# Reordering the first loads of a cross-layer kernel: the transposing load second on its queue, W0 on the other, no filler between the input halves

## The chip, the cores and the metric

One core of one Trainium2 chip runs the whole program. The metric is the time of one execution in microseconds on the device, with inputs and outputs in device memory. Fast runs of the kernel before spread over up to 1.5 per cent on one chip (131.16 to 133.06 us in 31 runs). Each run also lists the mean granted clock of TensorE over the span (1.00 is full). A run is called slow here when it took over 1.5 per cent longer than the fastest run of the same kernel; medians are of all runs, ratios of the fast ones alone.

## The reference

Six cross layers on a batch of 4096 rows with 416 features, in bf16:

```python
x = x0                                  # x0 [4096, 416]
for l in range(6):                      # ws [6, 416, 416], bs [6, 416]
    x = x0 * (x @ ws[l] + bs[l]) + x
```

## The kernel before: the parts that matter

Rows are processed in four slabs of 1024. Features are split into three chunks of 128 and a tail of 32. The activations are needed transposed (features on partitions). For slab 0 the first 512 rows come in plainly as two halves `xin` and are transposed on TensorE; rows 512 to 1023 come by one transposing DMA into `x0T_sb`. All of these first loads share two hardware queues (SP and ACT) and one software queue (POOL):

```python
# SP
sp.dma_start(xin_sb[:, 0:2, :], x0_v[:, 0:2, :]).then_inc(s_xin[0], 16)
sp.dma_start(w_sb[:, 0, 0, :], ws[0, 0:128, :]).then_inc(s_w0, 16)
sp.dma_start_transpose(x0T_sb[:, :, H:SB], x0[H:SB, 0:DF]).then_inc(s_x0T[0], 16)
for l in range(1, L):                       # W1 .. W5 and the tail rows of their weights
    ...
# ACT
act.dma_start(xin_sb[:, 2:4, :], x0_v[:, 2:4, :]).then_inc(s_xin[1], 16)
act.dma_start(w_sb[:, 0, 1:NC, :], ...).then_inc(s_w[0], 16)      # W0, blocks 2 and 3
act.dma_start(xtl_sb[:, 4:JS, :], ...).then_inc(s_xtl0, 16)       # tail input
act.dma_start(bsa_sb[1:L + 1, :], bs[:, :]).then_inc(s_bs, 16)    # bias rows
for g in (1, 3):
    load_wt(act, g, 0, 1, s_wt[0])                                # tail weights of layer 0
```

TensorE works through the start of layer 0 in program order: 13 filler matmuls (their results are not used), transposes of input half 0, three fillers, transposes of half 1, step k=0 (needs W0 block 1), step k=1 (needs W0 blocks 2 and 3), bias sums (need the bias rows), tail transposes (need the tail input), step k=2, then the tail group of matmuls, then half B of the slab (needs the transposing load):

```python
for k in range(NC):
    if k == 1:
        pe.wait_ge(s_w[0], 16)
    if k == 2:
        bias_sums()                  # waits for s_bs
        pe.wait_ge(s_xtl0, 16)
        tail_transposes(0)
    before_a(k)
    for m in range(NC):
        step(m, 0, k)
...                                  # tail group, then
pe.wait_ge(s_x0T[0], 16)
```

## Time and profile before

| | before |
|---|---|
| time, median of the first three runs | 131.67 us (131.44 to 132.03) |
| span of the profiled run, TensorE busy | 130.2 us, 125.0 us |
| first matmul of layer 0 | 6.10 us |
| first tail group (called T below) | 9.09 us |
| one layer afterwards | 4.88 us |
| W0 blocks 2 and 3: issue, landing | 1.34, 5.64 us |
| transposing load: issue, landing | 1.82, 9.02 us |

All moments are microseconds from the start of the span. A landing is the issue's start plus the time to landing that the DMA view gives. From T on the kernel keeps a fixed rhythm, so only the first ten microseconds are of interest here; the lines that show it stand in the prediction.

In the profile, PE is the row of TensorE's matmuls and PEld that of its weight loads; DVE is VectorE, ACT ScalarE, POOL GpSimd, SP SyncE, and a q behind a name marks what was issued to its DMA queue. One pair of lines belongs here because the prediction read another line in its place. This is the timeline of TensorE's matmuls in the kernel before (start, length, engine, line, operation; a bracket at the end would name an idle time and its releaser):

```profile
6.10 1.81 PE L194 MATMUL ps<-x0T_sb,w_sb 128*32 128x512 bf16 x24
7.84 0.26 PE L194 MATMUL ps<-u_sb,bsa_sb 7*32 7x6 bf16 x16
```

There is no bracket: the matmuls of k=0 and k=1 run until 6.10 + 1.81 = 7.91, and the bias sums follow without a gap (the profile models the ends of matmuls, hence the small overlap). No wait for the bias rows shows.

### The profile page before, as it was taken

The numbers are of one execution on the slowest core, as the hardware profiler recorded it, in microseconds if no ns is written. First come the engines' busy times: TensorE is split into PE (matmuls) and PEld (weight loads), VectorE is DVE, ScalarE is ACT, GpSimd is POOL, SyncE is SP. The second block draws the span as 40 slices with busy tenths as digits, with TensorE's granted clock in tenths as the row PEclk, the third lists the DMA queues.
The fourth block names the chain that finished last, engine by engine and source line by source line (L and its number), as shares of the span: only waits on it lengthen the run. The fifth ranks groups of instructions, "written<-read, shape, count | busy, mean of one in ns | idle before, by whom it ended". The sixth has DMA issues, their size and how long they took to land.

```text
span 130.2 us, 5402 instructions
## 1 busy us (share of the span) xinstructions
PE 125.0 (96%) x2456; PEld 65.0 (50%) x2456; DVE 99.6 (76%) x151; ACT 68.8 (53%) x157; POOL 21.9 (17%) x39
## 2 busy tenths in 40 slices
PE   6999999999999999999999999999999999999970
PEld 4655545545545545545545545545445545545540
DVE  2319779779779779779779779779779779779780
ACT  0615456566905456565905556565905555555680
POOL 7302012012022022012022022012022032012230
PEclk9999999999999999999999999999999999999999
DMA  3999799960009935000008534000009707000026
GB/s 100 232 264 352 77 202 221 162 146 0 5 3 105 158 106 167 5 0 5 0 5 161 106 111 156 0 5 0 5 0 118 154 0 262 5 0 5 0 86 184
DMA packets 34018, 11.95 MB, mean 92 GB/s; under 512 B 26694, under 2 KB 33996, under 8 KB 33996
## 3 DMA queue, kind: packets, MB, share of 16 engines
q1 hardware_dynamic: 32160, 10.91, 40.9%
q10 hardware_dynamic: 1708, 0.64, 1.9%
q8 instruction: 19, 0.31, 0.9%
q0 software_dynamic: 128, 0.06, 0.2%
q14 instruction: 3, 0.02, 0.1%
HBM read 2.90 MB, written 3.41 MB: 48 GB/s over the span
## 4 chain that ended last, share of the span: by engine, by line
PE 96%; ACT 0%; POOL 0%; issue 0%; POOLq 0%
PE ps L194 81%; PE ps L328 10%; PE ps L201 3%; PE ps L226 1%; PE ps L381 1%; ACT o_sb L503 0%; POOL ones_sb L153 0%; POOLq L522 0%
## 5 line engine op out<-in xcount | busy, mean ns | idle before, releaser
L427 DVE SCALAR_TENSOR_TENSOR xT_sb<-ps,cb_sb,x0T_sb 128x512 bf16<-128x512 f32 x120 | 80.9, 743 | 16.9 <-PE ps L328 16.9
L194 PE MATMUL ps<-xT_sb,w_sb 128*32 128x512 bf16 (+1 forms) x1680 | 89.3, 364 | 0.0
L194 PEld LDWEIGHTS ps<-xT_sb,w_sb 128*32 128x32 bf16 x1680 | 42.8, 97 | 38.7 <-issue 4.2
L475 ACT ACTIVATE t_sb<-ps,cb_sb 64x256 f32<-64x256 f32 x48 | 22.6, 470 | 35.6 <-PE ps L194 35.2
L457 ACT ACTIVATE xt_sb<-xt_sb 32x256 bf16<-32x256 bf16 x80 | 33.1, 414 | 14.4 <-POOL xt_sb L181 13.6
L181 POOL TENSOR_TENSOR xt_sb<-t_sb,x0t_sb 128x256 bf16<-128x256 f32 x20 | 13.5, 676 | 83.0 <-ACT t_sb L475 83.0
L194 PE MATMUL ps<-x0T_sb,w_sb 128*32 128x512 bf16 (+1 forms) x336 | 18.8, 369 | 0.0
L427 DVE SCALAR_TENSOR_TENSOR xo_sb<-ps,cb_sb,x0T_sb 128x512 bf16<-128x512 f32 x23 | 15.6, 744 | 3.4 <-PE ps L328 3.3
L194 PEld LDWEIGHTS ps<-x0T_sb,w_sb 128*32 128x32 bf16 x336 | 8.6, 98 | 7.9 <-issue 1.6
L328 PE MATMUL ps<-xt_sb,wt_sb 32*128 32x512 bf16 (+1 forms) x160 | 12.1, 326 | 0.0
L328 PE MATMUL ps<-xt_sb,wc_sb 32*128 32x256 bf16 x80 | 7.7, 268 | 0.0
L328 PEld LDWEIGHTS ps<-xt_sb,wt_sb 32*128 32x128 bf16 x160 | 2.4, 91 | 8.5 <-DVE xT_sb L427 8.5
L457 ACT ACTIVATE x0t_sb<-x0t_sb 32x256 bf16<-32x256 bf16 x12 | 5.0, 414 | 0.2
L181 POOL TENSOR_TENSOR xot_sb<-t_sb,x0t_sb 128x256 bf16<-128x256 f32 x4 | 2.7, 675 | 13.5 <-ACT t_sb L475 13.5
L201 PE MATMUL ps<-ones_sb 128*128 128x256 bf16 x16 | 3.8, 419 | 1.2 <-POOL ones_sb L153 1.2
L328 PEld LDWEIGHTS ps<-xt_sb,wc_sb 32*128 32x128 bf16 x80 | 4.0, 93 | 0.4
L405 DVE COPY x0T_sb<-ps 128x256 bf16<-128x256 bf16 x4 | 1.2, 292 | 3.3 <-PE ps L226 3.1
L446 ACT ACT_TABLE_LOAD x1 | 1.3, 1283 | 3.9 <-issue 3.9
L201 PEld LDWEIGHTS ps<-ones_sb 128*128 128x128 bf16 x16 | 2.2, 146 | 1.9 <-POOL ones_sb L153 1.2
L328 PE MATMUL ps<-x0t_sb,wt_sb 32*128 32x512 bf16 (+1 forms) x32 | 2.4, 326 | 0.0
L483 ACT ACTIVATE x0t_sb<-ps 64x256 bf16<-64x256 f32 x6 | 2.3, 378 | 0.1
L409 DVE CAST x0t_sb<-ps 128x256 bf16<-128x256 f32 x1 | 0.4, 425 | 2.1 <-PE ps L194 2.1
(38 smaller groups left out, 25.5 us busy)
## 6 DMA issues: line engine op xcount, KB each, us to landing
out_dram<-o_sb SPq DMA_DIRECT2D x3, 832.0 KB, 4.2
w_sb<-in_ws_dram SPq DMA_DIRECT2D x5, 312.0 KB, 4.6
out_dram<-o_sb SPq DMA_DIRECT2D x2, 256.0 KB, 2.5
xin_sb<-in_x_dram SPq DMA_DIRECT2D x1, 208.0 KB, 3.0
xin_sb<-in_x_dram ACTq DMA_DIRECT2D x1, 208.0 KB, 3.3
w_sb<-in_ws_dram ACTq DMA_DIRECT2D x1, 208.0 KB, 4.3
xtl_sb<-in_x_dram SPq DMA_DIRECT2D x1, 192.0 KB, 7.0
wt_sb<-in_ws_dram SPq DMA_DIRECT2D x2, 80.0 KB, 4.0
```

Of the source, the lines that this page charges most:

```text
L181: pool.tensor_tensor(out=dst, in0=t32_sb[:, n % 2, :], in1=x0t_sb[:, s, 0:G], op=ALU.mult).then_inc(s_xt, 1)
L194: return pe.matmul(dst, lhsT=lhsT, rhs=rhs, start=start, stop=True, skip_group_check=True, tile_position=(0, 32 * q),)
L201: pe.matmul(ps[:, 7, 0:256], lhsT=ones_sb[:, 0:128], rhs=ones_sb[:, :], start=True, stop=True)
L226: ins = pe.transpose(out=psT[:, IN_BANKS[h][c], (j % 2) * 128:(j % 2 + 1) * 128], in_=xin_sb[:, j, c * 128:(c + 1) * 128], identity=ident[ ...
L328: return pe.matmul(dst, lhsT=lhsT, rhs=srct[lane(g), cols], start=l == 0 and start, stop=True, skip_group_check=True, tile_position=(32 * ...
L381: return pe.transpose(out=psT[:, bank, slot * 128:(slot + 1) * 128], in_=xo_sb[:, NS - 1, c, j * 128:(j + 1) * 128], identity=ident[:, :],)
L405: dve.tensor_copy(out=x0T_sb[:, c, h * 256:(h + 1) * 256], in_=psT[:, IN_BANKS[h][c], 0:256]).then_inc(s_inD, 1)
L427: dve.scalar_tensor_tensor(out=dst, in0=ps[:, NC * half + c, :], scalar=cb_sb[:, c, l:l + 1], in1=x0T_sb[:, c, o:o + H], op0=ALU.add, op1= ...
L446: act.activation(out=x0T_sb[:, 1, h * 256:(h + 1) * 256], in_=psT[:, IN_BANKS[h][1], 0:256], func=ACTF.Copy).then_inc(s_inA, 1)
L457: ins = act.activation(out=buf[lane(g), G:2 * G], in_=buf[lane(g ^ 1), 0:G], func=ACTF.Copy)
L475: ins = act.activation(out=t32_sb[HALVES[h], n % 2, :], in_=tail(h), func=ACTF.Identity, bias=cb_sb[HALVES[h], NC, l:l + 1],)
L483: ins = act.activation(out=x0t_sb[HALVES[h], s + 1, 0:G], in_=spare(h), func=ACTF.Copy)
```

## The change

Its intent is to have the transposing load, the largest of the first loads, land earlier by issuing it as the second load of SP. W0's first block therefore goes to ACT, where the bias rows move to the end. With more issues on ACT, one PSUM copy moves from ACT to VectorE. The filler between the input halves goes. On POOL the small tail-by-tail weights are split by layer and follow the tail weights.

```diff
 # SP
-            sp.dma_start(w_sb[:, 0, 0, :], ws[0, 0:128, :]).then_inc(s_w0, 16)
             sp.dma_start_transpose(x0T_sb[:, :, H:SB], x0[H:SB, 0:DF]).then_inc(s_x0T[0], 16)
 # ACT
             act.dma_start(xin_sb[:, 2:4, :], x0_v[:, 2:4, :]).then_inc(s_xin[1], 16)
+            act.dma_start(w_sb[:, 0, 0, :], ws[0, 0:128, :]).then_inc(s_w0, 16)
             act.dma_start(w_sb[:, 0, 1:NC, :], ...).then_inc(s_w[0], 16)
             act.dma_start(xtl_sb[:, 4:JS, :], x0_v[:, 4:JS, DF:D]).then_inc(s_xtl0, 16)
-            act.dma_start(bsa_sb[1:L + 1, :], bs[:, :]).then_inc(s_bs, 16)
             for g in (1, 3):
                 load_wt(act, g, 0, 1, s_wt[0])
+            act.dma_start(bsa_sb[1:L + 1, :], bs[:, :]).then_inc(s_bs, 16)
 # TensorE, after the transposes of half h
-                fill((3, 0)[h])
 # VectorE copies of half 0: chunks (0, 2) -> (0, 1, 2); ACT keeps only chunk 1 of half 1
-                            pe.wait_ge((s_inD, s_inA, s_inD)[k], (3, 2, 4)[k])
+                            pe.wait_ge((s_inD, s_inA, s_inD)[k], (4, 1, 5)[k])
 # POOL: wc load split into layer 0 and layers 1 to 5, after the tail weights; TensorE waits for it by layer  (cut)
```

## The prediction

> **What bounds the kernel now.** I read the busy table first, then the chain of work that ended last, then the waits of the first 14 us, then the timeline and DMA issues of that stretch. The first two, from the page:
>
> ```profile
> PE 125.0 (96%) x2456; PEld 65.0 (50%) x2456; DVE 99.6 (76%) x151; ACT 68.8 (53%) x157; POOL 21.9 (17%) x39
> ...
> PE 96%; ACT 0%; POOL 0%; issue 0%; POOLq 0%
> ```
>
> TensorE is busy nearly all the time and is 96% of the chain that ends last. The chain in order of time shows where layer 0 hands over to a regular rhythm:
>
> ```profile
> 5.41 0.64 PE ps L226 x6
> 6.10 3.00 PE ps L194 x67
> 9.09 0.56 PE ps L328 x8
> 9.66 4.33 PE ps L194 x84
> 13.98 0.55 PE ps L328 x8
> 14.53 4.33 PE ps L194 x84
> ```
>
> Columns: start, length, what. From the first tail group (9.09) on, each layer takes 4.89 us (13.98 - 9.09, and 18.86 - 13.98 = 4.88 later), which the diff does not touch. So the change moves the end only by what it moves that 9.09. I call this moment T. The waits before it, each with total, count and longest in us:
>
> ```profile
> DVE x0t_sb L409 <- PE ps L194: 2.1, 1, 2.1
> ACT cb_sb L450 <- PE ps L194: 1.9, 1, 1.9
> ...
> PEld ps L194 <- DMA bsa_sb<-in_bs_dram: 0.4, 1, 0.4
> PEld ps L328 <- ACT x0t_sb L461: 0.4, 1, 0.4
> ```
>
> There is one DMA wait on the PE path before T: the bias rows. The timeline around it (start, length, engine, line, operation, then idle before and releaser):
>
> ```profile
> 2.39 0.66 ACTq L441 DMA_DIRECT2D bsa_sb<-in_bs_dram  x1
> 3.07 0.80 ACTq L107 DMA_DIRECT2D wt_sb<-in_ws_dram  x2
> ...
> 7.84 0.17 PEld L194 LDWEIGHTS ps<-u_sb,bsa_sb 7*32 7x32 bf16 x16 [0.42 <-DMA bsa_sb<-in_bs_dram]
> ...
> 8.51 0.38 ACT L461 ACTIVATE x0t_sb<-ps 128x256 bf16<-128x256 f32 x1
> ...
> 9.02 0.14 PEld L328 LDWEIGHTS ps<-x0t_sb,wt_sb 32*128 32x128 bf16 x8 [0.42 <-ACT x0t_sb L461]
> ```
>
> Bias rows issued at 2.39 release PE at about 7.84, so 5.4 us. From there everything is a chain: bias sums, tail transposes, the ACT copy 8.51 to 8.89, tail weights at 9.02. T follows the landing of the bias rows by 1.2 us (9.02 - 7.84).
>
> Last, the issues to landing, from DMA views of narrow stretches (size, us):
>
> ```profile
> xin_sb<-in_x_dram ACTq DMA_DIRECT2D x1, 208.0 KB, 3.3
> w_sb<-in_ws_dram ACTq DMA_DIRECT2D x1, 208.0 KB, 4.3
> xtl_sb<-in_x_dram ACTq DMA_DIRECT2D x1, 32.0 KB, 4.6
> wt_sb<-in_ws_dram ACTq DMA_DIRECT2D x1, 8.0 KB, 4.9
> wt_sb<-in_ws_dram ACTq DMA_DIRECT2D x1, 8.0 KB, 5.3
> x0T_sb<-in_x_dram SPq DMA_TRANSPOSE x1, 7.2
> ```
>
> Everything issued after 1.7 us takes about 5 us, even 8 KB: the small loads stand in a backlog, of which the transposing load (issued 1.82, landed 9.02) is the largest part.
>
> **What the Trainium skill says.** "DMA: Bandwidth & Descriptors", section "Issuing engines are not separate DMA queues": loads from SP, ACT and POOL run on the same 16 DMA engines and interleave; a second issuing engine saves only issue time. The trace agrees: an 8 KB load of ACT takes 4.9 us and a 16 KB one of POOL 5.0 to 5.1. The same page, section "Queues, rings and completion order": an engine takes its rings in turn by packets and each ring in order. The order within ACT's ring is visible (input, W0, tail input, bias, tail weights land in issue order); the fair turn is not, since POOL's almost empty ring waits as long.
> "TensorE: Matmul & The Clock Gate", Part 1: the array runs at half rate until it has been busy for a free-running window of about 3.4 us. The trace agrees: six 128-column transposes take 0.64 us, 107 ns each (the page's cold figure), and the four-way 512-column groups of layer 0 start about 0.40 us apart (weight loads at 6.07, 6.48, 6.87) and then 0.21. It became fast near 6.9 us.
>
> **The change part by part.**
> 1. The filler between the halves goes: three matmuls, 0.64 us in the chain (4.77 to 5.41). The second input half landed at 0.82 + 3.3 = 4.12, so its transposes can follow at 4.77 and end at 5.41, not 6.05: 0.64 us earlier on PE.
> 2. The half-0 chunk-1 copy moves from ACT to VectorE. VectorE now has five copies of 0.29 us. Chunk 0 starts at 4.38 as before; back to back the fourth, which step k=0 needs, ends at 4.38 + 4 x 0.29 = 5.55, the fifth at 5.84. Before, k=0 waited for the third copy, at 5.66 + 0.29 = 5.95, and began at 6.10. So k=0 can begin near 5.7: a gain of 0.4 us, not 0.64.
> 3. W0's first block moves from SP to ACT, behind the input. Landed at 1.33 + 3.0 = 4.33; now it shares the engines with the transpose for longer, and I expect 4.8 to 5.5, just in time for 5.7. The two other blocks, 1.34 + 4.3 = 5.64 before, go to about 6.3; k=1 wants them at 6.9. ACT's own table load (1.28 us) starts after its last issue, at 4.4 instead of 3.9, its remaining copy ends near 6.1: also ahead of k=1.
> 4. The transposing load is issued 0.49 us earlier (1.33), landing near 8.5 instead of 9.02. PE asks for it at about 9.6. No wait on it is shown, so nothing gained now, only slack.
> 5. The bias rows go behind W0's block (0.49 us) and both tail-weight issues (0.80 us): 2.39 + 1.29 = 3.68. The last small load of that kind issued late (3.45) took 5.3 us, and ahead of 3.68 stands most of the transpose, whose issuing takes 2.73 us (now until 4.06). With 5.1 us they land at 8.8, against 7.84: 0.95 us later. This is on the path.
> 6. The lane-weight loads split in two and stand behind POOL's tail weights: 4 x 0.67 us of issue, from 2.5 to 5.2. Layer 0's pair, issued by 3.8, lands by 8.8; layer 1's has until 14. The small select for the bias sums moves from 4.08 to 5.2, still early. Cost: nothing.
>
> The sum: k=0 and k=1 start 0.4 us earlier and only wait longer for the bias rows (parts 1 and 2 give nothing). T = 8.8 + 1.2 = 10.0 in place of 9.02: +0.95 us. Then the fixed rhythm. 131.67 + 0.95 is 132.6; I take 132.5, since a backlog with W0's and the input's bytes unchanged may let the bias rows through a little sooner.
>
> **The rivals.**
> A. The intended gain: the bias rows are not late because the ACT ring's last load finds the transpose further along, or rings are served fairly. If they land by 7.4, PE never waits and the whole 0.4 us (at most 0.64) is kept: 131.1 to 131.3. For it: the transpose starts half a microsecond earlier. Against: no small load of any queue got through in under 4.6 us.
> B. The clock: without filler PE idles some 0.3 us before k=0 and 1 us or more at the bias wait. If the window then counts as idle, the array stays slow for one more window of 3.4 us; half of that is lost, up to 1.7 us, on top of the 0.95: 134.3. Against: most of each window remains busy (about 70% of 7 to 10.2), and no slow stretch after 6.9 is in the trace before.
> C. The transpose starves W0: the second and third blocks land at 7.5 or later and step k=1 waits. That stays hidden under the wait for the bias rows unless it passes 8.1 (8.8 less the 0.64 us of a fast k=1): no more than 0.5 us extra, 133.
>
> **Range and chances.** The main step gives +0.6 to +1.2 (latency of 4.75 to 5.35 us); A takes the low end to 131.2, B and C the high end to 133.7. The three runs before span 131.44 to 132.03, so the noise is near 0.3 us. Two per cent is 2.63 us: a gain of that size exceeds all of the stretch that can be saved (0.64), a loss needs the backlog and a cold clock together. Faster 0.01, same 0.93, slower 0.06. Prediction 132.5 us, range 131.2 to 133.7.
>
> **What would show it.** Part 1 and 2: layer 0's first matmul near 5.7 instead of 6.10. Part 5: the bias weight load starts near 8.8 with an idle of over 1 us put down to the bias DMA. The first tail group near 10.0, then layers 4.88 us apart. Part 4: transposing load landing near 8.5 with no wait on it. The clock: groups of layer 0 0.21 us apart from about 7 us. I am wrong if the bias rows land before 8.0, if PE waits for W0 or the transpose instead, or if the layer rhythm after T is not 4.88.

## The result, and the profile after

The changed kernel took 136.72 us (median; 135.35 to 138.00, 4 runs, of which the one at 138.00 is slow) against 131.65 us (131.44 to 132.03, 4 runs). The ratio is 1.0347, with a 95% interval of 1.0266 to 1.0428: slower. Ratios here are the mean time of one kernel's fast runs over that of the other's fast runs of the same rounds, so not quite the ratio of the medians quoted.

The chain that ended last, in order of time, of the changed kernel (start, length, what):

```profile
4.11 5.86 DMA bsa_sb<-in_bs_dram
10.02 2.11 PE ps L194 x39
12.12 0.97 PE ps L328 x8
13.10 5.55 PE ps L194 x72
18.64 0.55 PE ps L328 x8
19.19 4.33 PE ps L194 x84
```

T moved from 9.09 to 12.12, the next tail group from 13.98 to 18.64; after that the rhythm is the old one. All of the loss lies ahead of 18.64: 18.64 - 13.98 = 4.66 us, and the spans differ by 134.9 - 130.2 = 4.7. A load now heads this chain. The waits of the first 14 us (total, count, longest):

```profile
PEld ps L194 <- DMA w_sb<-in_ws_dram: 2.4, 1, 2.4
PE ps L194 <- DMA w_sb<-in_ws_dram: 1.9, 1, 1.9
...
PEld ps L194 <- DMA bsa_sb<-in_bs_dram: 1.3, 1, 1.3
...
PE ps L194 <- DMA bsa_sb<-in_bs_dram: 0.5, 1, 0.5
```

Now the matmul row (PE) waits too: 1.9 us for W0 and 0.5 us for the bias rows. In these times TensorE computes nothing. The DMA view of the stretch 1.6 to 2.3 us shows why (size, us from issue to landing):

```profile
w_sb<-in_ws_dram ACTq DMA_DIRECT2D x1, 208.0 KB, 6.4
w_sb<-in_ws_dram ACTq DMA_DIRECT2D x1, 104.0 KB, 3.1
wt_sb<-in_ws_dram POOLq DMA_DIRECT2D x2, 16.0 KB, 5.1
x0T_sb<-in_x_dram SPq DMA_TRANSPOSE x1, 6.9
```

W0's first block still lands 3.1 us after its issue (1.32 to 4.42), but blocks 2 and 3, issued at 1.86, need 6.4 us (4.3 before) and land at 8.26. What went over the engines in the half microsecond after 4.0 us is plain from the DMA view of that window, by queue: packets, MB, share of 16 engines (the times of packets are added up, so a share can pass 100%). First the kernel before, then the changed one (q1 is SP, q10 is ACT, as their byte counts show):

```profile
q10 hardware_dynamic: 353, 0.15, 109.3%
q0 software_dynamic: 6, 0.00, 2.0%
q1 hardware_dynamic: 9, 0.00, 1.9%
```

```profile
q1 hardware_dynamic: 500, 0.13, 114.3%
q0 software_dynamic: 28, 0.02, 10.1%
q10 hardware_dynamic: 5, 0.00, 1.3%
```

Before, ACT moved 353 packets (W0 and the tail input) in that window and SP 9. Changed, SP moves 500 packets of some 260 bytes, the transposing load, and ACT 5.

The last part is the clock. Stretches of the changed kernel, with columns for each engine's busy time (and number of instructions), then granted clock, DMA share and GB/s:

```profile
6.00:8.00 2.00, 0.41 (x8) 0.00 (x0) 0.00 (x0) 0.40 (x2) 0.00 (x0) 1.00 1.29 228
8.00:10.00 2.00, 1.14 (x12) 0.23 (x12) 0.00 (x0) 0.00 (x0) 0.00 (x0) 0.68 1.24 254
10.00:12.00 2.00, 1.99 (x44) 0.93 (x44) 0.42 (x1) 0.57 (x2) 0.00 (x0) 0.50 1.09 314
12.00:14.00 2.00, 2.00 (x32) 1.05 (x32) 0.75 (x2) 0.02 (x1) 0.00 (x0) 0.50 1.31 260
14.00:16.00 2.00, 2.00 (x28) 0.83 (x24) 1.98 (x4) 1.13 (x3) 0.67 (x1) 0.61 1.04 104
```

TensorE stood idle most of 6 to 8 us; the clock then fell to one half and came back near 15.5 us. In the kernel before it does not fall, as in the same stretch there:

```profile
10.00:12.00 2.00, 2.00 (x44) 1.00 (x40) 2.00 (x4) 0.94 (x2) 0.67 (x1) 1.00 1.11 358
```

This prices the two parts in this pair of profiles. The bias sums begin at 10.02 instead of 7.84: 2.18 us of waiting. From there to the second tail group the profile has 18.64 - 10.02 = 8.62 us instead of 13.98 - 7.84 = 6.14, with TensorE busy throughout: 2.48 us from the slow clock. Together 4.66.

### The profile page after: what moved, and what is told of

It is laid out like the page before. It is cut to its first block, busy times and chain, and to the rows that moved or that the text cites. A ratio compares the mean times of both kernels' runs of the same rounds, so it can differ in the third digit from the quotient of the medians.

```text
span 134.9 us, 5399 instructions
## 1 busy us (share of the span) xinstructions
PE 127.1 (94%) x2453; PEld 65.0 (48%) x2453; DVE 99.8 (74%) x152; ACT 68.3 (51%) x156; POOL 22.8 (17%) x41
## 3 DMA queue, kind: packets, MB, share of 16 engines
HBM read 2.90 MB, written 3.41 MB: 47 GB/s over the span
## 4 chain that ended last, share of the span: by engine, by line
PE 90%; DMA 4%; ACTq 2%; ACT 0%; issue 0%
PE ps L194 79%; PE ps L328 10%; DMA bsa_sb<-in_bs_dram 4%; ACTq L107 1%; PE ps L381 1%; ACT o_sb L503 0%; ACTq L439 0%; ACTq L441 0%; ACTq L438 0%; ACTq L440 0%
## 5 line engine op out<-in xcount | busy, mean ns | idle before, releaser
L194 PE MATMUL ps<-x0T_sb,w_sb 128*32 128x512 bf16 (+1 forms) x336 | 20.9, 396 | 2.0 <-DMA w_sb<-in_ws_dram 1.9
L328 PE MATMUL ps<-xt_sb,wt_sb 32*128 32x512 bf16 (+1 forms) x160 | 12.1, 326 | 0.0
L201 PE MATMUL ps<-ones_sb 128*128 128x256 bf16 x13 | 3.0, 419 | 1.2 <-POOL ones_sb L152 1.2
L328 PE MATMUL ps<-x0t_sb,wt_sb 32*128 32x512 bf16 (+1 forms) x32 | 2.9, 372 | 0.0
```

What stands on the lines that cost most here:

```text
L194: return pe.matmul(dst, lhsT=lhsT, rhs=rhs, start=start, stop=True, skip_group_check=True, tile_position=(0, 32 * q),)
L201: pe.matmul(ps[:, 7, 0:256], lhsT=ones_sb[:, 0:128], rhs=ones_sb[:, :], start=True, stop=True)
L328: return pe.matmul(dst, lhsT=lhsT, rhs=srct[lane(g), cols], start=l == 0 and start, stop=True, skip_group_check=True, tile_position=(32 * ...
```

## The experiments

Theory 1: the transposing load, queued right behind the input, takes the DMA engines from W0 on ACT's queue; TensorE then waits for W0 and for all that stands behind it, and its clock may fall while it is idle. Rivals: the place of the bias rows; the missing filler; ACT's queue simply being too long with all of W0 in it; W1 coming in earlier. The experiments ran in three jobs on three chips, each with runs of the kernel before, to which the ratios refer. The results together first. "W0" is the landing of blocks 2 and 3, "bias" the start of the bias sums, T the first tail group in the chain, all in us from the profiled run.

| run | median us | ratio (95% interval) | W0 | bias | T |
|---|---|---|---|---|---|
| before | 131.65 | 1 | 5.6 | 7.8 | 9.1 |
| changed | 136.72 | 1.0347 (1.0266 to 1.0428) | 8.3 | 10.0 | 12.1 |
| after_w0_front | 133.08 | 1.0071 (1.0034 to 1.0108) | 4.9 | 8.7 | 10.0 |
| before_order_only | 135.23 | 1.0240 (1.0182 to 1.0298) | 9.3 | 10.1 | 11.6 |
| after_fill_waits | 135.07 | 1.0235 (1.0188 to 1.0282) | 8.5 | 10.6 | 11.9 |
| after_bs_early | 134.97 | 1.0198 (1.0134 to 1.0262) | 8.4 | 9.1 | 11.6 |
| after_tr_held | 131.25 | 0.9953 (0.9932 to 0.9973) | 5.7 | 7.1 | 8.4 |
| after_w1_held | 134.97 | 1.0211 (1.0165 to 1.0257) | 8.4 | 9.2 | 11.3 |
| after_plain | 133.34 | 1.0082 (1.0053 to 1.0110) | 6.4 | 8.9 | 10.2 |
| before_no_fill | 131.95 | 0.9993 (0.9968 to 1.0018) | 5.1 | 6.9 | 8.7 |
| before_tr_held | 131.25 | 0.9945 (0.9919 to 0.9971) | 5.2 | 7.6 | 8.9 |
| before_bs_last | 132.71 | 1.0042 (1.0019 to 1.0066) | 5.0 | 9.1 | 10.3 |
| after_again | 136.10 | 1.0221 (1.0147 to 1.0295) | 8.3 | 10.5 | 12.6 |

In these jobs the kernel before had medians of 132.04 to 132.13 us. All results are correct except after_plain, which is wrong on purpose. All profiles are of fast runs except that of after_again: its run took 136.24 us, 1.6 per cent over the fastest of that job, so its moments stand here for comparison only. One caution for the last two columns: the array came to full speed at 4.1 to 7.0 us, at a different moment in every profile (the last section has the records), so a few tenths of a microsecond of T in a single profile are luck.

### Only W0's first block put back (after_w0_front)

```diff
+ sp.dma_start(w_sb[:, 0, 0, :], ws[0, 0:128, :])      # SP, ahead of the transposing load
- act.dma_start(w_sb[:, 0, 0, :], ws[0, 0:128, :])
```

> Changed kernel with one thing undone: W0's first block is again the second load of SP, ahead of the transposing load. Theory 1 (the transposing load, queued directly behind the input, takes the DMA engines from ACT's W0 blocks): W0's last two blocks land near 5.7 us instead of 8.26, no W0 wait on PE, the bias rows at about 8.7, no slow clock after 8 us: 132.0 to 132.8 us. Rival (the bias rows at the end of ACT's queue and the missing filler are the cause): the slow stretch stays and the time is 134.5 or more.

W0 landed at 4.9 us, the wait for it is gone, the clock stayed full, and most of the loss went with it: 133.08 us, 0.3 above the range. What is left is a true wait for the bias rows (timeline of TensorE):

```profile
5.46 1.48 PE L195 MATMUL ps<-x0T_sb,w_sb 128*32 128x512 bf16 x24
8.73 0.26 PE L195 MATMUL ps<-u_sb,bsa_sb 7*32 7x6 bf16 x16 [1.79 <-DMA bsa_sb<-in_bs_dram]
```

Bias sums at 8.73 are what the prediction had worked out (8.8), in part by luck: the rows were issued at 3.42, not 3.68, and took 5.27 us, not 5.1. T at 9.98 and the loss of 0.7 per cent fit its sum as well. The sum was thus right for a kernel in which W0 comes in time, and that kernel is not the changed one.

### Only the queue order changed (before_order_only)

```diff
- sp.dma_start(w_sb[:, 0, 0, :], ws[0, 0:128, :])      # in the kernel before
+ act.dma_start(w_sb[:, 0, 0, :], ws[0, 0:128, :])     # second on ACT
```

> The kernel before with the queue order alone changed: W0's first block moves from SP to ACT behind the input, so the transposing load is second on SP. Filler, bias rows ahead of the tail weights, copies and lane weights as before. Theory 1: W0's last two blocks land near 8 us, PE waits about 1.5 to 2 us for them, the array turns slow again: 134.0 to 136.5 us. Rival (filler and bias order are the cause): under 132.3 us.

135.23 us, as theory 1 had it: the order alone makes most of the loss, with filler and bias order as before. The wait for W0 was longer than expected, 2.79 us on the matmul row:

```profile
9.32 0.83 PE L193 MATMUL ps<-x0T_sb,w_sb 128*32 128x512 bf16 x12 [2.79 <-DMA w_sb<-in_ws_dram]
```

In the profiled run the clock nevertheless stayed at 1.00 after it, apart from the end of the kernel; two of the other three runs had mean clocks of 0.981 and 0.986 and took 135.63 and 135.80 us, against 134.53 us with 1.000. A wait of this length can bring the slow clock; it need not.

### Filler in the two waits (after_fill_waits)

```diff
  if k == 1:
+     fill(16, 6)                  # into a bank free at that point
      pe.wait_ge(s_w[0], 16)
  if k == 2:
+     fill(8, 6)
      bias_sums()
```

> Changed kernel with filler matmuls on PE in its two waits (16 before the wait for W0's last blocks, 8 before the wait for the bias rows), loads untouched. Theory 1 with the slow clock as its second half (2.2 us of waiting, 2.5 us of slow clock): the bias rows still land near 10 us, but the array stays fast, the first tail group at about 11.2, time 133.6 to 134.4 us. Rival (the clock fell for another reason, or it costs little): 136 us or more, slow stretch still there.

The slow stretch is gone: 1.00 in every stretch from 6 to 14 us, as in this one:

```profile
10.00:12.00 2.00, 1.95 (x56) 1.09 (x57) 0.42 (x1) 0.57 (x2) 0.00 (x0) 1.00 1.10 309
```

T came only to 11.88, since in this run the bias sums began at 10.62 rather than 10.02, and the time missed its range by 0.7 us. The layer after T is again of normal length: 16.77 - 11.88 = 4.89 us, against 6.52 in the changed kernel. So the filler does what it should to the clock, but the times do not show clearly what it is worth (see after_again).

### The bias rows earlier (after_bs_early)

```diff
+ act.dma_start(bsa_sb[1:L + 1, :], bs[:, :])          # ahead of the tail weights again
  for g in (1, 3):
      load_wt(act, g, 0, 1, s_wt[0])
- act.dma_start(bsa_sb[1:L + 1, :], bs[:, :])
```

> Changed kernel with the bias rows issued ahead of ACT's tail weights again, loads otherwise as changed. Theory 1: W0 still lands near 8.3 us and PE waits for it; the bias rows land 0.5 to 1 us earlier (9.0 to 9.5), the clock still falls: 135 to 136.5 us. My predicted main step alone (bias order is the cost): under 132.8 us.

134.97 us, 0.03 below the range of theory 1 and far above the 132.8 of the prediction's step alone. The bias sums start at 9.13, right behind k=1; W0 is awaited 1.77 us (1.94 in the changed kernel) and the clock falls (0.50 between 10 and 12 us). The place of the bias rows is not the main cause.

### The transposing load held back (after_tr_held)

```diff
+ sp.wait_ge(s_w0, 16)             # W0's first block has landed
  sp.dma_start_transpose(x0T_sb[:, :, H:SB], x0[H:SB, 0:DF])
```

> Changed kernel, SP holds the transposing load until W0's first block has landed (about 4.4 us), everything else as changed, so ACT still carries all of W0 and the bias rows last. Theory 1 (the transposing load takes the engines from ACT's queue from about 4 us on): W0's last blocks land near 5.3 us, bias rows by 8, no slow clock; the transposing load now lands at 9.5 to 10.5 and sets the pace: 131.6 to 133.0 us. Rival (ACT's queue is simply too long with all of W0 in it): W0 still lands after 7 us and the time is over 134.

One wait turns the changed kernel from 2.2 to 3.5% slower (after_again and the first result) into 0.5% faster, better than expected. ACT still carries all of W0, so ACT's queue is not too long by itself. DMA issues of the first 12 us of this run:

```profile
w_sb<-in_ws_dram ACTq DMA_DIRECT2D x1, 208.0 KB, 3.8
...
wt_sb<-in_ws_dram ACTq DMA_DIRECT2D x2, 8.0 KB, 3.2
...
x0T_sb<-in_x_dram SPq DMA_TRANSPOSE x1, 3.9
```

W0 takes 3.8 us instead of 6.4, the 8 KB loads of ACT 3.2 instead of 5.9 to 6.3. The transposing load is issued 3.04 us later (4.37 instead of 1.33), but it then needs 3.9 us instead of 6.9: it lands at 8.27 against 8.23. Being early gained it nothing.

### W1 and the rest held back (after_w1_held)

```diff
  sp.dma_start_transpose(x0T_sb[:, :, H:SB], x0[H:SB, 0:DF])
+ sp.wait_ge(s_w[0], 16)           # all of W0 has landed, then W1 .. W5
```

> Changed kernel, SP holds W1 and all that follows until W0's last blocks have landed; the transposing load stays second. Theory 1 (the transposing load itself): W0 still lands at 7.5 to 8.5 us, PE waits for it over 1.2 us: 134 to 136.5 us. Rival (the shorter issue of the transposing load, 1.53 instead of 2.73 us, lets W1 and the lane weights of layers 1 to 5 in 1.7 us earlier, and they delay W0): W0 lands near 6 us, time under 133.3.

W0 lands at 8.4 us and the time is 134.97 us: W1 is not what holds W0 up. In the half microsecond after 4.0 us ACT moved 23 packets and SP 465, with nothing behind the transposing load on SP. That load by itself is enough to delay W0. The bias sums came at 9.2, though, for 10.0 in the changed kernel, so the loads behind it may have cost the bias rows something; that was not tested further.

### The same bytes without the transpose (after_plain)

```diff
- sp.dma_start_transpose(x0T_sb[:, :, H:SB], x0[H:SB, 0:DF])
+ for c in range(NC):              # wrong result on purpose: same rows, runs of 256 bytes
+     sp.dma_start(x0T_sb[:, c, H:SB].rearrange("p (a b) -> p a b", b=128), ...)
```

> Changed kernel with the transposing load replaced by three plain loads of the same rows and bytes in runs of 256 bytes (wrong result on purpose: nothing is transposed). If any 393 KB of small packets ahead on SP hold W0 up: W0 lands at 7 to 8.5 us and the time is 133.5 to 136.5. If the transposing as such is what holds ACT's queue: W0 lands before 6.2 us, no W0 wait on PE, 131.5 to 133.2 us.

W0 lands at 6.36 us, between the two expectations: 0.7 us later than with the transposing load held back (5.67), 1.9 us earlier than with it in front (8.26). Bytes ahead on the other queue cost something; most of the delay is gone with the transposing load. The edit changes one thing more: SP issued three loads over 2.00 us in place of one over 1.53 us. So whether the transposing as such or the pauses between the issues made the difference is not separated. The wait for W0 on the matmul row is 0.2 us, and the bias rows, last on ACT, account for most of the rest (1.6 us), which puts the time at 133.34 us. Two of its ten runs were slow, at 135.36 and 135.63 us with a mean clock of 0.987: the clock may fall here too. In the half microsecond after 4.5 us ACT moved 163 packets here and 86 in the changed kernel. How the engines share their time between the queues is not seen in the trace and stays open.

### The filler alone (before_no_fill)

```diff
- fill((3, 0)[h])                  # in the kernel before
```

> The kernel before without the three fillers between the input halves, nothing else. My prediction's part 1 with the bias rows governing: layer 0 starts near 5.5 us and waits longer for the bias rows, first tail group unchanged at 9.0, 131.3 to 132.3 us. Rival (the filler keeps the clock up): a slow stretch shows and the time is over 133.

No change of time (0.9993, interval 0.9968 to 1.0018), and no slow stretch. The profile corrects the prediction's reading of the kernel before: with the bias rows issued at the same 2.38 us, the bias sums now start at 6.91, with no wait on the matmul row. So those rows had landed by then, in 4.5 us or less, and in the kernel before they did not set T. TensorE's own work did. T comes to 8.65 here and is then held by a tail weight of POOL. Of the 0.93 us by which the bias sums came earlier, layer 0's earlier start gives 0.60 (5.50 for 6.10); the rest goes with the moment from which the array was fast, 5.34 us in this profile and 6.82 in that of the kernel before.

### The held transposing load in the kernel before (before_tr_held)

```diff
- fill((3, 0)[h])
+ sp.wait_ge(s_w0, 16)
  sp.dma_start_transpose(x0T_sb[:, :, H:SB], x0[H:SB, 0:DF])
```

> The kernel before with two edits: no filler between the input halves, and SP holds its transposing load (still third) until W0's first block has landed. If holding that load is what made the held version of the changed kernel fast: all small loads land within about 3.5 us of issue, the transposing load in about 4 us, near 8.3, first tail group at 7.8 to 8.3 and 130.8 to 131.4 us, as good as the held version of the changed kernel or slightly better (ACT's copies come 0.5 us earlier). Rival (the gain needs all of W0 on ACT): 131.8 us or more.

131.25 us, 0.9945: as good as the held version of the changed kernel, so the gain does not need the reordering. Again the transposing load takes 3.9 us (7.2 before) and the small loads 3.3 to 3.8. T is later than expected (8.86) in the profiled run, in which the groups of k=0 and k=1 started about 0.4 us apart, that is at half speed, until 7 us. The two held versions are the fastest of the study; they cannot be told apart.

### The bias rows last, alone (before_bs_last)

```diff
- act.dma_start(bsa_sb[1:L + 1, :], bs[:, :])          # in the kernel before
  for g in (1, 3):
      load_wt(act, g, 0, 1, s_wt[0])
+ act.dma_start(bsa_sb[1:L + 1, :], bs[:, :])
```

> The kernel before with one edit: ACT issues the bias rows after its tail weights (issue near 3.3 us). This is the main step of my prediction alone. By that step they land at 8.3 to 8.6 and PE truly waits for them: 132.4 to 133.1 us. If the reading behind it was wrong and bias rows were never late: within 0.3 us of before.

132.71 us, ratio 1.0042: inside the range. The rows are issued at 3.42 and awaited until 9.08, a wait of 1.4 us on the matmul row, T 1.25 us later than before in these profiled runs. The main step of the prediction exists and is worth about half a per cent (0.58 us between the medians).

### The changed kernel on the same chip (after_again)

> The changed kernel itself, on the same chip as the others, to compare with the versions run there. 135 to 138 us as recorded, W0's last blocks landing after 8 us, the bias rows near 10, and the clock below full in most runs. If the chip makes a difference, less.

W0 lands at 8.26, the bias sums begin at 10.54 and the clock falls, as recorded; the median is 136.10 us. The time of the changed kernel depends on its clock from run to run: over both jobs the runs in the fast state took 134.12 us at 0.997, 135.96 at 0.983, 135.35 at 0.980, 136.64 at 0.975 and 136.80 at 0.971. Two more, at 136.24 and 136.72 us, are slow by the rule above, with clocks of 0.985 and 0.983, which lie within those of the fast runs. The run with the nearly full clock is 2.0 us above the median before of its job (132.13), close to the 2.18 us of waiting read from the first trace. Since the two fast runs of this job average about what after_fill_waits took on another chip, the share of the slow clock in the typical loss isn't settled by times: 2.5 of 4.7 us in the profiled run, and from nothing to somewhat more than that from run to run.

## Why the prediction was wrong, point by point

- **The bound and the rhythm**: right. After T, both kernels need 4.88 us a layer, and the whole loss is in T and the layer after it.
- **Parts 1 and 2** (filler and copies): right that layer 0 starts earlier, at 5.58 for 5.7, and that this gains nothing in the changed kernel.
- **Part 3** is the step that failed: "The two other blocks, 1.34 + 4.3 = 5.64 before, go to about 6.3; k=1 wants them at 6.9." They landed at 8.26. The step added 0.66 us, little more than the 0.52 us by which the block put ahead delays their issue (1.34 to 1.86), and charged nothing for the transposing load that SP now issues ahead of them, although I had called that load the largest part of the backlog. Holding it back brought W0 to 5.67 with ACT's queue unchanged. The first block, expected at 4.8 to 5.5, landed at 4.42: the delay fell on the loads behind it.
- **Part 4** (the transposing load lands near 8.5): right, 8.23; it had slack, but was put ahead of loads that had none.
- **Part 5** (bias rows at 8.8, +0.95 us): right where W0 is in time (bias sums at 8.73 in after_w0_front). In the changed kernel they were issued at 4.11 and took 5.86 us, for 3.68 and 5.1; the two tail-weight issues ahead of them took 1.21 us, for 0.80, and the issue of the transposing load 1.53, for 2.73. The reading behind it was wrong all the same: the idle of 0.42 on the weight-load row was taken for a wait. The same 0.42 stands there in before_tr_held with "issue" as its releaser, and in the kernel before ahead of the tail group with ACT's copy; the matmul row and the chain had no DMA in them.
- **Part 6**: right, as far as the waits of the changed kernel show: none for the small lane weights.
- **Rival C** was the right mechanism with a wrong limit. "No more than 0.5 us extra" took the bias rows' landing as fixed at 8.8, but whatever delays W0 delays what stands behind it on the same queue.
- **Rival B** was right in kind and came on top: idle time brought the slow clock, which was gone when filler took its place (after_fill_waits); 2.48 us in the profiled run, where I allowed 1.7 and thought it unlikely. The slow clock lasted 6.83 us, not the one window of 3.4. I had set the two rivals side by side, B behind the wait for the bias rows; the wait for W0 that C describes can bring B about.

## What to carry to other kernels

In this kernel a load that had slack was better issued late than early: in front of urgent loads it slowed them on the other queues too (8 KB on ACT took 5.9 to 6.3 us for 3.2, 16 KB on POOL 5.1 for 3.3) and landed no sooner (8.23 and 8.27 us). Ask of every early load what it takes the engines from, on the other queues too, and try holding a large transposing load back with a wait on an urgent load, here W0's first block. Before calling a load a bound, look for the wait on the matmul row and in the chain, and count an idle TensorE twice: for the wait, and for the clock that may fall after it.

## What the Trainium skill lacked or had wrong

- "DMA: Bandwidth & Descriptors", section "Queues, rings and completion order", says that an engine takes the queue rows it has work for in turn, packet by packet. Beside the transposing load, ACT's queue, with W0 issued 1.7 us earlier and not landed, moved 5 packets in half a microsecond while SP moved 500. Either the turn was not an even one in that stretch, or W0's packets did not yet stand before the engines; the trace does not show which.
- The same page, section "Rules for kernel authors", says "A transpose next to ordinary DMAs needs nothing". That concerns correct data, and no result here speaks against it. For time the page lacks that ordinary loads of 8 KB took 5.9 to 6.3 us beside the transposing load and 3.2 us ahead of it, and 208 KB took 6.4 and 3.8.
- The same page, section "Anatomy of one DMA — SWDGE (gpsimd) path", fits a POOL load with about 2.0 us plus bytes over 436 GB/s; for 16 KB that is 2.04 us (an estimate from that formula). The runs show 5.0 to 5.1 in the kernel before and 3.3 in after_tr_held. None of these loads ran alone, so this does not test the fit; what the page lacks is the price of company.
- "TensorE: Matmul & The Clock Gate", Part 1, lets the clock fall after at least one idle window of about 3.4 us. The clock records of the packed traces agree with the window's length: full from 5.32 us, half from 8.73, full from 15.56 in the changed kernel (3.41 and 6.83 us apart); 6.12, 9.53, 12.95 in after_bs_early; 6.03, 9.44, 12.86 in after_w1_held. But a window need not be idle throughout. If one counts on from the first record in steps of 3.41 us, the windows after which the clock fell held 1.79 to 2.24 us of idle matmul row (four profiles), and none with 1.74 us or less brought a fall; 1.80 (before_order_only) and 1.84 (after_w0_front) did not either. So the limit lay near half a window in these runs, and the idle time in one window counts, not the length of one wait: the 2.79 us of before_order_only were cut by the edge at 8.07, the 1.94 us of the changed kernel were not. Once it had fallen, it came back after a window with at most 0.12 us idle; in the changed kernel the next window still held 0.53, and it stayed at half for one more. This is read from single profiles, with modelled ends of matmuls, and was not tested.
- The same Part 1 warns that recorded clock events are not to be trusted fully; the page doesn't have the trap met here. The first record comes at 4.05 (after_again) to 6.96 us (before_tr_held), and until then the views read 1.00 although the array runs at half rate: the 256-column fillers stand 213 ns apart and 128-column transposes 107 ns, against 56 ns for transposes after the record (after_again, before_order_only).
